# Reading a turned tile back from memory in quarters instead of halves

## The chip, the cores and the metric

The kernel runs on one core of a Trainium2 chip. The metric is the time of one execution in microseconds (us) on the device. The core has a matrix engine (PE, with weight loads shown as a row of their own, PEld), a vector engine (DVE), a scalar engine (ACT), a general engine (POOL), and a queue processor (SP) that issues DMA transfers and computes nothing. Transfers run on 16 DMA engines that all queues share.

## The reference, cut to what matters

```python
# attention: batch 8, heads 8, sequence 576, head size 64
scores = scale * q @ k.T
thresh = max(scores) - tau                      # along each row
scores = where(scores >= thresh, scores, -1e9)
attn   = softmax(scores)
x      = (attn @ v) as (4608, 512)              # tokens x (heads * 64)
# bilinear feed-forward: d_ff 1536
out    = ((x @ w_a) * (x @ w_b)) @ w_out
```

All of it is float32.

## The kernel before, in words

**Units and slots.** Two heads of one batch element form a pair; there are 32 pairs. A pair's 576 query rows are cut into four blocks of 128 rows (u = 0 to 3) and a rest of 64 rows; the rests of two neighbouring pairs are handled together as one block (u = 4, called NT). Each (pair, u) is a unit; there are 144 of them. The main loop runs over slots g = 0 to 146. In slot g the scores of unit g are made on PE (`scores`, line 404), reduced on DVE (line 411), exponentiated on ACT (432), masked and summed on DVE (435) and normalised on ACT (454).

**Turning the weights.** For attn @ v the weights must stand with the keys on the partitions. From slot 9 on this is done in two steps. DVE transposes within blocks of 32x32 (line 502). Then the blocks are exchanged through a buffer in device memory: in slot g `turn_blocks` posts four transfers of 144 KB that write unit g-1 to the buffer `swap` (shown as `swap<-tw`, one for each group of 32 partitions), and `turn_back` posts the transfers that read unit g-2 back into a tile `wT` (shown as `wT<-swap`). There are two `wT` tiles. Group y of the tile is read from block y of the buffer, which one of the four writes filled. Before it posts the reads, `turn_back` issues whatever is still waiting of that unit's writes (`flush`). The rests of units (NT) are read back by transfers of 144 KB of their own.

**Product.** `weighted` multiplies two units of a pair with v (`product`, line 546: 72 matmuls over two `wT` tiles, each of which reads from all four groups of one tile). It runs three slots after the second unit of the two. ACT and DVE copy the result out (553, 554), and the results of four pairs together are the input of the feed-forward, whose matmuls (lines 750, 854, 920) fill the slots between the attention parts. The order of PE's instructions is written out by the loop; `advance` hands out a number of columns of feed-forward work at fixed places of a slot.

**The queue of transfers.** Up to slot 36 `post` issues a transfer at once (line 144). From slot 37 on (`state["paced"]`) it appends it to a list, `bulk`, and transfers of the kinds "tw" and "wT" are put ahead of loads and stores that were posted in this slot or the one before. `passed` counts the columns that PE has been given, and takes the next entry from the list when the count has reached zero. An entry then costs 320 columns for each 36864 elements (144 KB) that it moves, rounded down, so that a load of k or q (under 144 KB) costs nothing. `pump` (line 157) issues the entry on SP, its first transfer behind the PE instruction last written, so that SP waits for that instruction's end. What is left in the list when a consumer is written is issued by `flush` without such a wait. SP executes strictly in order.

**Loads.** Four slots ahead of a pair's first unit its k is posted (four transfers of 72 KB), two slots ahead DVE transposes it (line 365); q follows in two parts, v in four transfers. They have the lower priority described above.

Of the kernel before, what the change touches and what calls it, by code (L numbers as in the profile page):

```python
# [54 lines left out]
def kernel(  # L55
# [57 lines left out]
    G = P // Q  # L113
# [25 lines left out]
    def post(key, *moves):  # L139

        if not state["paced"]:
            for move in moves:
                state["turn"] += state["over"]
                (nc.scalar if state["turn"] % 2 else nc.sync).dma_start(*move)  # L144
        else:
            at = len(bulk)
            if key[0] in ("tw", "wT"):
                while at and bulk[at - 1][0][0] not in ("tw", "wT") and bulk[at - 1][1] >= state["slot"] - 1:
                    at -= 1
            bulk.insert(at, (key, state["slot"], moves))  # L150
# [13 lines left out]
    def flush(*keys):  # L164

        while any(key in keys for key, _, _ in bulk):
            pump(1, False)
# [68 lines left out]
    for F in range(NF):  # L236
# [3 lines left out]
    state = {"loaded": 0, "added": 0, "converted": 0, "rows": 0, "sums": False, "through": 0, "over": False,  # L240
             "layer": False, "paced": False, "all": False, "turn": 0, "due": NPIECES, "wide": True, "slot": 0, "reading": False, "first": 0}
# [113 lines left out]
    prepared, scored, weights, turned, whole = {}, {}, {}, {}, {}  # L355
# [111 lines left out]
    def turned_tile(here=None):  # L467
        if here == (0, NT):
            return sums_sb[:, NSUM - TURNED:].rearrange("p (g s e) -> p g s e", g=G + 1, s=NSLOT)
        return work.tile([P, G + 1, NSLOT, Q], FP32, tag="wT", bufs=2, name="wT")  # L470
# [46 lines left out]
    def turn_back(i, u):  # L517

        key = "wT", i, min(u // 2, 1) if i >= HP else u // 2
        if u < NT or i < HP:  # L520
            flush(("tw", i, u))
            swap = swaps.pop((i, u)).rearrange("g p e -> p g e")
            turned[i, u] = turned_tile((i, u))
            for y in range(0, G, 2):
                post(key, (turned[i, u][:, y:y + 2].rearrange("p g s e -> p g (s e)"), swap[:, y:y + 2]))
        if i >= HP and u == (3 if i % 2 else NT):
            flush(("tw", i - i % 2, NT))
            swap = swaps[i - i % 2, NT].rearrange("g p e -> p g e")
            for y in range(2):
                post(key, (turned[i, 2 + y][:, G].rearrange("p s e -> p (s e)"), swap[:, i % 2 * 2 + y]))  # L530
            if i % 2:
                del swaps[i - 1, NT]
# [579 lines left out]
    n = 0  # L1112
# [4 lines left out]
    for g in range(len(units) + PV_LAG):  # L1117
# [9 lines left out]
        if BY_PE + 1 < g <= len(units) + 1:  # L1127
            n = g - PV_LAG
            back = (1 if BY_PE <= n and parts(*units[n]) else 0,)
            if not back[0] or units[g - 2] == (0, NT):  # L1130
                turn_back(*units[g - 2])
        if here:
            i, u = units[g]
# [38 lines left out]
        if g > BY_PE:  # L1172
            n = g - PV_LAG
            held = 0.0
            now = parts(*units[n]) if BY_PE <= n < len(units) else []
            if now:
                held = 384 - (PORTIONS[2] + PORTIONS[3]) * pace + NSLOT * sum(width(*x) for x in now) // 2
                held = min(max(held, 0.0), 384)
            advance(PORTIONS[1] * pace - held)
            for p in range(HP, NPR):  # L1180
                for name, d in (("k", 2),):
                    if g == (second if False else first)[p] - d:
                        prep(p, name)
            for p, h in now:
                if pairs[p][1] == 0:
                    make_x(2 if h == 1 and p >= HP and pairs[p][0] % GT == 0 else 1)
                make_room()
                weighted(p, h)
                passed(NSLOT * width(p, h) // 2)
                running["owed"] -= NSLOT * width(p, h) // 2  # L1190
            if back and back[0] > 0 and units[g - 2] != (0, NT):
                turn_back(*units[g - 2])
# [89 lines left out]
```

## Time and profile before

| | us |
|---|---|
| runs | 1406.40 (median), 1405.77, 1414.82 |
| profiled execution, whole | 1400.57 |
| its span, first to last instruction | 1398.8 |
| PE busy | 1361.5 |
| DVE busy | 1013.9 |
| ACT busy | 680.8 |

The profile is of one execution. "Busy" counts the time in which an engine has an instruction under way; PE's share says that it is nearly always occupied, not that it is at its peak. An entry of the waits names who waited, the line, who ended the wait, the total in us, how often, and the longest. SP computes nothing, so all of its rows are issues and waits, and its engine name carries a q (SPq). A row of an operation has the number of instructions and the shortest, median and longest duration in nanoseconds.

The transfers that the change touches run between 310 us (slot 37) and 1251 us. Of the reads into `wT` in that stretch, 194 move 288 KB and 50 move 144 KB (the rests).

### The profile page before, as it was taken

The numbers are of one execution on the slowest core, as the hardware profiler recorded it, in microseconds if no ns is written. First come the engines' busy times: TensorE is split into PE (matmuls) and PEld (weight loads), VectorE is DVE, ScalarE is ACT, GpSimd is POOL, SyncE is SP. The second block draws the span as 40 slices with busy tenths as digits, with TensorE's granted clock in tenths as the row PEclk, the third lists the DMA queues.
The fourth block names the chain that finished last, engine by engine and source line by source line (L and its number), as shares of the span: only waits on it lengthen the run. The fifth ranks groups of instructions, "written<-read, shape, count | busy, mean of one in ns | idle before, by whom it ended". The sixth has DMA issues, their size and how long they took to land.

```text
span 1398.8 us, 76307 instructions
## 1 busy us (share of the span) xinstructions
PE 1361.5 (97%) x33836; PEld 1258.5 (90%) x33836; DVE 1013.9 (72%) x2205; ACT 680.8 (49%) x1248; POOL 492.8 (35%) x675
## 2 busy tenths in 40 slices
PE   7889999999999999999999999999999999999998
PEld 5677588999998799999999999998899998799998
DVE  6999877787777768786767776778777776745425
ACT  6977555545554555544454545454545455431110
POOL 2764543424150607060515142332515060708100
PEclk9999999999999999999999999999999999999999
DMA  9977876667666775676556775566656775550000
GB/s 211 241 212 223 204 206 173 174 170 187 174 154 168 190 192 155 176 190 160 143 143 160 186 180 159 136 190 169 181 130 161 199 190 154 137 146 19 4 19 18
DMA packets 327449, 223.21 MB, mean 160 GB/s; under 512 B 171600, under 2 KB 311632, under 8 KB 327120
## 3 DMA queue, kind: packets, MB, share of 16 engines
q1 hardware_dynamic: 323936, 216.95, 60.1%
q8 instruction: 266, 4.36, 1.3%
q10 hardware_dynamic: 3184, 1.38, 0.4%
q14 instruction: 63, 0.52, 0.1%
HBM read 128.58 MB, written 89.65 MB: 156 GB/s over the span
## 4 chain that ended last, share of the span: by engine, by line
PE 88%; DMA 5%; DVE 4%; SPq 2%; issue 1%; ACT 1%; ACTq 0%; DVEq 0%
PE pab L750 29%; PE po L920 22%; PE pab L854 18%; PE sc L404 9%; PE pv L546 9%; SPq L144 1%; DMA vm<-in_v_dram 1%; DMA wT<-swap 1%; DVE tw L435 1%; DVE mx L411 1%; DMA more_u<-in_moe_w_a_dram 1%; DVE low L311 0%; DMA more_u<-in_moe_w_b_dram 0%; DVE tw L502 0%; DMA sums_u<-in_k_dram 0%
## 5 line engine op out<-in xcount | busy, mean ns | idle before, releaser
L454 ACT ACTIVATE tw<-tw,rcp 128x576 f32<-128x576 f32 x272 | 196.1, 768 | 201.3 <-DVE rcp L448 201.3
L411 DVE TENSOR_REDUCE mx<-sc 128x1 f32<-128x576 f32 x288 | 204.6, 752 | 121.2 <-PE sc L404 120.9
L432 ACT ACTIVATE tw<-sc,bias,scalars 128x576 f32<-128x576 f32 x288 | 239.6, 832 | 10.4 <-DMA qT<-in_q_dram 0.4
L712 POOL TENSOR_TENSOR h<-h,u 128x512 f32<-128x512 f32 x28 | 35.2, 1277 | 590.4 <-DVE h L824 414.1
L435 DVE SCALAR_TENSOR_TENSOR tw<-sc,thr,tw 128x576 f32<-128x576 f32 x288 | 220.9, 797 | 12.3 <-ACT tw L432 11.9
L920 PE MATMUL po<-wo_sb,h 64*64 64x256 f32 (+1 forms) x3408 | 210.5, 367 | 0.0
L502 DVE STREAM_TRANSPOSE tw<-tw 128x576 f32<-128x576 f32 x272 | 194.4, 752 | 0.8 <-ACT tw L454 0.8
L920 PEld LDWEIGHTS po<-wo_sb,h 64*64 64x64 f32 x3408 | 169.8, 133 | 14.9
L404 PE MATMUL sc<-kT,qT 64*64 64x288 f32 x2016 | 170.3, 404 | 1.8 <-issue 0.9
L546 PE MATMUL pv<-wT,vm 64*64 64x128 f32 (+2 forms) x4896 | 164.0, 275 | 3.7 <-DMA vm<-in_v_dram 1.4
L546 PEld LDWEIGHTS pv<-wT,vm 64*64 64x64 f32 x4896 | 153.2, 133 | 12.0 <-issue 4.0
L920 PE MATMUL po<-sums_u,h 64*64 64x256 f32 x2448 | 156.6, 376 | 0.0
L883 POOL TENSOR_TENSOR h<-h 128x256 f32<-128x256 f32 x168 | 117.2, 731 | 110.9 <-PE po L920 106.1
L750 PE MATMUL pab<-xU,wb_sb 64*64 64x128 f32 x4352 | 137.8, 269 | 0.0
L920 PEld LDWEIGHTS po<-sums_u,h 64*64 64x64 f32 x2448 | 126.1, 133 | 12.3 <-DVE h L862 0.5
L750 PEld LDWEIGHTS pab<-xU,wb_sb 64*64 64x64 f32 x4352 | 133.3, 133 | 1.8 <-ACT h L806 0.5
L404 PEld LDWEIGHTS sc<-kT,qT 64*64 64x64 f32 x2016 | 108.8, 133 | 17.3 <-issue 4.9
L431 ACT ACTIVATE bias<-mx,scalars 128x1 f32<-128x1 f32 x288 | 82.7, 287 | 66.1 <-DVE mx L411 65.6
L553 ACT COPY xT<-pv 128x128 f32<-128x128 f32 (+1 forms) x68 | 17.6, 259 | 193.5 <-PE pv L546 193.5
L750 PE MATMUL pab<-xS,wa_sb 64*64 64x128 f32 x2176 | 108.5, 269 | 0.8 <-issue 0.8
L554 DVE COPY xT<-pv 64x128 f32<-64x128 f32 (+1 forms) x136 | 38.1, 280 | 80.5 <-PE pv L546 79.0
L535 ACT COPY kept<-po 128x512 f32<-128x512 f32 x65 | 34.8, 535 | 120.3 <-PE po L920 106.4
(163 smaller groups left out, 2468.7 us busy)
## 6 DMA issues: line engine op xcount, KB each, us to landing
wT<-swap SPq DMA_DIRECT2D x242, 288.0 KB, 3.8
swap<-tw SPq DMA_DIRECT2D x480, 144.0 KB, 3.1
vm<-in_v_dram SPq DMA_DIRECT2D x128, 72.0 KB, 2.6
swap<-tw SPq DMA_DIRECT2D x128, 72.0 KB, 2.9
kT<-in_k_dram SPq DMA_DIRECT2D x112, 72.0 KB, 3.2
wT<-swap SPq DMA_DIRECT2D x56, 144.0 KB, 3.6
out_dram<-kept SPq DMA_DIRECT2D x27, 256.0 KB, 3.7
qT<-in_q_dram SPq DMA_DIRECT2D x112, 40.0 KB, 2.8
```

The lines of the kernel that those rows point to most:

```text
L404: nc.tensor.matmul(sc[m][o * D:o * D + wide, c], qT[r, q0:q0 + wide], kT[r, c * SH:(c + 1) * SH], start=True, stop=True)
L411: nc.vector.tensor_reduce(mx[:, c], sc[j], axis=AX.XY, op=ALU.max)
L431: nc.scalar.activation(bias[:, j:j + 1], mx[:, j:j + 1], AF.Copy, scale=e_nscale)
L432: nc.scalar.activation(wb[j], sb[j], AF.Exp, bias=bias[:, j:j + 1], scale=e_scale)
L435: nc.vector.scalar_tensor_tensor(out=wv, in0=sb[j], scalar=thr[:, j:j + 1], in1=wv, op0=ALU.is_ge, op1=ALU.mult, accum_out=sums[:, j:j + 1])
L454: nc.scalar.activation(w, w, AF.Copy, scale=rcp[:, j:j + 1])
L502: nc.vector.transpose(w, w)
L546: nc.tensor.matmul(pv[c * D:(c + 1) * D, y], vm[rows, s], wT[y](rows, s), start=(s == 0), stop=(s == NSLOT - 1))
L750: nc.tensor.matmul(out[c * D:(c + 1) * D, r, f * P:(f + 1) * P], w[g][k][rows, w0:w0 + D], moving[k][rows], start=(fresh and k == 0 and f ...
L854: nc.tensor.matmul(pab[c:c + columns(), r], w[rows, f // n, k, fs + c:fs + c + columns()], moving, start=(k == 0), stop=(k == H - 1))
L883: (nc.vector if state["over"] else nc.gpsimd).tensor_tensor(*a, **kw)
L920: nc.tensor.matmul(po[c * D:(c + 1) * D, r, y, cut], ht[rows, t0:t0 + D], other[rows, f, cut], start=(f == 0), stop=(f == NF // 2 - 1))
```

## The change

Inside `turn_back`, from slot 37 on, each of the four groups of a unit's tile is read back by a transfer of its own (144 KB) and posted as an entry of its own; up to slot 36 two groups go together as before (288 KB). The entries of the rests are as they were. Each entry costs 320 columns in place of 640, and each brings its own wait for a PE instruction.

```diff
             flush(("tw", i, u))
             swap = swaps.pop((i, u)).rearrange("g p e -> p g e")
             turned[i, u] = turned_tile((i, u))
-            for y in range(0, G, 2):
-                post(key, (turned[i, u][:, y:y + 2].rearrange("p g s e -> p g (s e)"), swap[:, y:y + 2]))
+            n = 1 if state["paced"] else 2
+            for y in range(0, G, n):
+                post(key, (turned[i, u][:, y:y + n].rearrange("p g s e -> p g (s e)"), swap[:, y:y + n]))
         if i >= HP and u == (3 if i % 2 else NT):
```

## The prediction

> **What bounds the kernel now.** I read the page first, then the stretch that the change touches (310 us, slot 37, to 1262 us, the last product) by windows, then the waits of PE and of SP in that stretch, then the rows of the tiles wT and kT and of line 546. The page's first part says which engine is full:
>
> ```profile
> PE 1361.5 (97%) x33836; PEld 1258.5 (90%) x33836; DVE 1013.9 (72%) x2205; ACT 680.8 (49%) x1248; POOL 492.8 (35%) x675
> ```
>
> That is a mean over stages. The windows give the stretch itself (length, then busy time of PE, PEld, DVE, ACT, POOL, the granted clock, the DMA engines' share, GB/s):
>
> ```profile
> 310.00:500.00 190.00, 188.93 (x4859) 171.08 (x4854) 146.89 (x327) 99.97 (x181) 70.94 (x109) 1.00 0.69 179
> 500.00:700.00 200.00, 199.57 (x5089) 193.20 (x5085) 148.25 (x327) 97.32 (x176) 68.50 (x104) 1.00 0.64 166
> 700.00:900.00 200.00, 199.32 (x5234) 195.49 (x5228) 143.22 (x315) 97.42 (x175) 58.58 (x86) 1.00 0.62 162
> 900.00:1100.00 200.00, 198.98 (x5129) 186.67 (x5125) 149.99 (x330) 101.56 (x184) 70.28 (x108) 1.00 0.65 168
> 1100.00:1262.00 162.00, 160.92 (x4183) 146.98 (x4178) 109.05 (x240) 72.79 (x133) 52.01 (x77) 1.00 0.59 159
> ```
>
> PE is busy for 188.93 + 199.57 + 199.32 + 198.98 + 160.92 = 947.7 of 952 us, at a granted clock of 1.00. Its idle time in the stretch is 4.3 us. The rest of PE's idle time (1398.8 - 1361.5 - 4.3 = 33 us) lies before 310 us or after 1262 us, where the change does nothing. The 4.3 us are the first bound on any gain. Busy is not the same as at its peak, but the long pieces of the chain that ended last run evenly (128 matmuls of line 920 in 6.91 us twice, 54.0 ns each), so little is hidden in them.
>
> SP is the queue that the change loads. Its waits in the same stretch:
>
> ```profile
> SPq L157 <- DVE tw L502: 112.0, 54, 6.5
> SPq L157 <- PE pab L750: 105.8, 162, 3.6
> SPq L157 <- PE po L920: 85.3, 144, 3.0
> SPq L157 <- PE pab L854: 54.0, 88, 3.8
> SPq L157 <- PE sc L404: 36.3, 54, 2.3
> SPq L157 <- DMA swap<-tw: 16.9, 32, 1.7
> ```
>
> These six rows are 410 us of 952 in which SP stood still because something was not ready yet: 43% of the stretch. Mostly it is ahead of the work, and held back on purpose by its PE markers.
>
> **The change part by part.**
>
> *More issues on SP.* 194 transfers of 288 KB become 388 of 144 KB: 194 issues more, two for each of 97 units. What one costs:
>
> ```profile
> L157 SPq DMA_DIRECT2D swap<-tw x480: 303/396/2307, 313.4 to 1242.1; - x160
> L157 SPq DMA_DIRECT2D wT<-swap x244: 326/382/1687, 310.4 to 1250.9; - x122
> ```
>
> The writes of 144 KB have a median of 396 ns, the reads (four in five of 288 KB) 382 ns: an issue costs the same whatever it moves. With the semaphore instruction and the gaps between, SP's timeline has four such writes in 1.78 us (834.12 us), 0.445 us each. So 194 x 0.445 = 86 us more, or 0.89 us for each unit of about 9.8 us (952 / 97). Against 410 us of waiting that fits, and 324 us would be left. Everything behind the reads in SP's order (the next unit's writes, k, q, v, the stores) can slip by up to 0.89 us in a unit, until SP comes to the next marker that it has to wait for. In the slot at 1116 us the four writes of 144 KB behind the reads take 3.32 us in place of 1.78, because one of them waits for PE's scores; such a wait swallows the 0.89 us whole, and k comes after it. Cost on the path: 0. If that cover were gone, see the first rival.
>
> *Later markers.* The first group goes at the same column as before, the second 320 columns later than it went, the third at the same column, the fourth 320 later. Columns pass at four matmuls per 128: line 750 runs 312 matmuls in 8.66 us (27.8 ns each), so 320 columns are 0.28 us. Where the count jumps by 576 columns behind the scores, or by 1152 behind a product, two or more entries go on one marker, so not every quarter has a marker to itself. The reader of the tile is the product. Against each product's start I set the landing, read issue by issue from the trace, of the last read that had landed: the smallest distances in the stretch are 1.1 us (1104.3) and 1.6 us (1088.5), the typical one 5 us. The last quarter is later by 0.28 us and 0.89 us of issuing at most, 1.2 us, and moves half the bytes. Only the tightest product can be touched at all. Cost: 0, with an upper end of about 0.1 us.
>
> *The transfers themselves.* Bytes, run lengths (1152 bytes) and the order of the bytes stay. The issues of the stretch show how little the size does to one transfer:
>
> ```profile
> wT<-swap SPq DMA_DIRECT2D x194, 288.0 KB, 3.7
> wT<-swap SPq DMA_DIRECT2D x50, 144.0 KB, 3.6
> ```
>
> 3.7 us to landing for 288 KB, 3.6 us for 144 KB: nearly all of it is a fixed delay or time in a queue. The Trainium skill ("DMA: Bandwidth & Descriptors", Anatomy of one DMA, and Rules for kernel authors) says the same more sharply, and against this change: each DMA pays about 2.0 us whatever it moves, and transfers are to be joined into larger ones. By its figure, if nothing overlapped, 194 more would be 388 us; this trace has several in flight at any time, so I do not add that.
>
> *A finer wait for the writes.* A half reads two blocks of the buffer and waits for both writes; a quarter waits for one. At 1113.7 us the first half went once the second write had landed, 1.3 us after the first one. So the first quarter can go earlier, and only the last waits for the last write. This is a gain where reads hang on writes; SP's waits for writes are 16.9 us in all, yet in PE's waits of the stretch no wT stands at all:
>
> ```profile
> PE pab L750 <- issue: 2.1, 5, 0.8
> PE pv L546 <- issue: 1.1, 2, 0.7
> PE sc L404 <- DVE xt L554: 0.5, 1, 0.5
> PE sc L404 <- DVE xT L554: 0.3, 1, 0.3
> ```
>
> So it ends at most 4.3 us, at least 0. I take 0.5 us gained, nearest to the two short waits that end with DVE.
>
> *More semaphores ahead of a product.* A product now depends on eight reads in place of four.
>
> ```profile
> L546 PEldq EVENT_SEMAPHORE  x131: 51/51/1900, 317.8 to 1257.4; - x131
> ```
>
> 131 such instructions stand before 49 products, 51 ns each at the median, two waits in an instruction at most in the trace. Four more waits are two more instructions: 98 x 51 ns = 5.0 us if all of it showed. The 131 that are there (6.7 us) show at most as the 2.6 us of "issue" before line 546's weight loads; matmuls queued ahead hide them. I take 0.
>
> *k comes later.* This is what is late next:
>
> ```profile
> DMA kT<-in_k_dram: 2.1, 4
> ```
>
> That is DVE's transpose of k (line 365), which waited four times in 22, the longest 0.80 us. By landings, 11 of the 22 have under 2 us to spare. If these all slipped by 0.89 us, what exceeds their spare time adds up to 4.4 us; by twice that, 11.7 us. Once such a wait reached PE: DVE waited 0.72 us at 1106.8, the copies of line 554 came late, and PE's scores lost 0.46 us at 1108.7. I take two more of that kind, 1 us; ends 0 and 12 us.
>
> **Sum.** 0 + 0 + 0 - 0.5 + 0 + 1 = +0.5 us on an execution of 1400.57 us (span 1398.8 and 1.8 around it). The runs' median is 1406.4, 5.8 us above that execution, so I forecast 1407 by the runs' scale.
>
> **The rivals.**
>
> *SP falls behind (slower).* In the slots crowded with k, q, v and stores, the two extra issues are not absorbed, and each slot's writes, and with them the next reads, start late. The place is SP's order between a unit's reads and the next marker; the price is 0.89 us for each slot in which SP does not stand still between; it decides once SP's waits in a slot are under 0.89 us. For it: the kT row above, and SP's timeline from 780 to 797 us, which has hardly a pause between groups of issues. Against it: 410 us of waits, 4.2 us per unit. If a quarter of the 97 units pay, 24 x 0.89 = 21 us: 1428. The rule of the Trainium skill named above ("DMA: Bandwidth & Descriptors") would come out on this side.
>
> *The finer wait pays (faster, but little).* All reads that hang on writes come early, kT with them, and PE's 4.3 us go: 1402. For it: the reads at 1113.7 us. Against it: PE waits for no wT.
>
> *The semaphores show (slower by little or more).* 5 us, and as much again if each also holds up the weight load behind it: 1411 to 1416.
>
> *It does nothing of the kind it says.* Markers coincide, quarters go in pairs as before, and only issues are added: 1406, inside the forecast.
>
> **How the numbers follow.** No change, with the last rival in it, has 0.59; the finer wait 0.14; SP behind 0.19; the semaphores 0.08. One per cent (14 us) is about what a measurement of this kernel can tell from no change, as its three runs span 9 us. Faster by over 1% would need three times PE's idle time: 0.03, taken from the finer wait. Slower by over 1% (above 1420.5): SP behind, and a small part of the semaphores, 0.21. Within: 0.76. The low end is the finer wait's 1402 less 3 us for a lucky set of runs, 1399; the high end takes in the semaphores, the 12 us of k and the lower part of SP behind: 1424.
>
> **What would show it.** Right: 388 reads of 144 KB beside the rests at about 0.38 us per issue; SP's waits of line 157 down by some 86 us; PE still busy for 947 us or so of the stretch; kT's waits a few us at most. Wrong: rows of PE waiting for wT, vm or DVE after kT; a stretch that is longer than 952 us by more than PE's busy time explains; or many more "issue" waits before line 546.

## The result and the profile after

The changed kernel takes 1420.31 us (median of 7 runs, 1415.89 to 1423.13); the kernel before takes 1406.40 us (7 runs, 1403.06 to 1414.82). The two medians are 13.9 us apart; the ratio on record, taken over the runs, is 1.0079, with a 95% interval of 1.0056 to 1.0103: about 11 us slower. A second comparison on another occasion gave 1.0088 (1.0058 to 1.0118). The change is slower by a little under 1%.

The profiled execution took 1416.46 us with a span of 1414.7 us, 15.9 us above the one of before (which, with 1400.57 us, lies below all seven runs above). To see where these are, I cut both spans at the same two matmuls, the first and the last of the stretch in which the change acts. The windows (length, busy time of PE, PEld, DVE, ACT, POOL, clock, DMA share, GB/s) of the kernel before and of the changed one:

```profile
306.20:1261.20 955.00, 950.73 (x24522) 896.54 (x24515) 699.84 (x1543) 471.23 (x850) 320.09 (x481) 1.00 0.64 167
```

```profile
306.80:1274.20 967.40, 956.29 (x24518) 905.24 (x24514) 700.57 (x1542) 470.47 (x850) 320.08 (x481) 1.00 0.64 165
```

The same work takes 967.4 in place of 955.0 us: 12.4 of the 15.9 us. Another 0.6 us lie ahead of the stretch and 2.9 us behind it, where the two programs are the same; those I put down to the two executions. The DMA engines' share and rate hardly moved. PE's idle time went from 4.3 to 11.1 us, and its busy time grew by 5.6 us although it does the same matmuls. So PE's idle time shows little more than half of the loss.

A part of the growth of busy time is the clock. The 1.00 of the windows is rounded; in the changed kernel's stretch there is one phase of 3.4 us at half clock, right behind an idle time of PE of 2.09 us:

```profile
817.80:821.20 3.40, 3.40 (x35) 2.35 (x34) 1.50 (x4) 1.44 (x2) 0.00 (x0) 0.50 0.80 200
```

The stretch of the kernel before has none. 3.4 us at half clock are 1.7 us lost, and the longest matmuls of line 404 (684 ns, 454 before) stand in this phase. The profiles of the experiments below with two markers, with the change and an early k, with k ahead of the second unit's reads without the change, and of the change once more have five more such phases in the stretch. All six begin 0.1 to 1.3 us after the end of an idle time of PE of 2.0 to 4.0 us. Four idle times of 2.2 to 2.6 us have none behind them, so not every one brings it. The other 3.9 us of the growth are not traced; matmuls that are counted as busy while they wait may be among them.

What ended the waits of PE in the stretch (engine, line, who ended the wait, us, times, longest; line numbers behind the change have moved by one):

```profile
PE sc L404 <- DVE xt L555: 2.8, 2, 2.6
PE sc L404 <- DVE xT L555: 2.2, 2, 2.1
PE sc L404 <- DVE h L816: 1.8, 1, 1.8
PE pv L547 <- issue: 1.5, 3, 0.7
```

PE waits for DVE, at the scores. And DVE, of all things that come from memory, waits for k:

```profile
DVE kT L365 <- DMA kT<-in_k_dram: 17.0, 8, 3.0
```

Before, this row was 2.1 us in four waits. One of the eight, from the chain of work that ended last (start, length, what):

```profile
807.03 5.16 DMA wT<-swap
812.19 0.02 issue
812.21 0.02 SPq L157
812.22 0.03 issue
812.25 3.71 DMA kT<-in_k_dram
...
816.08 0.78 DVE kT L365
...
817.62 2.10 PE sc L404 x13
```

SP's last issue of k came at 812.25 us, k landed 3.71 us later, DVE could transpose it at 816.08, the copies of the product behind the transpose came late, and PE's scores started at 817.62 after an idle time of 2.09 us.

Set unit by unit against the kernel before, by the end of each unit's scores, PE falls behind in four places: by 2.7 us up to 512 us of the changed kernel (two waits for k, at 475 and 491 us), by 3.9 us at 820 to 830 us (the wait above, with the 1.7 us of half clock), by 2.3 us at 963 us and by 2.1 us at 1124 us. Together these are 10.9 of the 12.4 us. The other three of the eight waits for k (626, 794 and 980 us) cost PE nothing that can be seen; the rest of the 12.4 us is steps of under 1 us in both directions.

SP itself waits less than before, but is far from full:

```profile
SPq L157 <- PE pab L751: 106.5, 188, 3.3
SPq L157 <- PE po L921: 76.3, 151, 2.9
SPq L157 <- DVE tw L502: 68.6, 26, 5.9
SPq L157 <- PE pab L855: 56.2, 89, 3.6
...
SPq L157 <- DMA swap<-tw: 0.4, 1, 0.4
```

All rows of line 157 together are 346 us, against 416 us before. Waits for landings of transfers fell too, from 18.1 us to 2.2 us, and a load of k takes 3.3 us from issue to landing in both kernels; so it is not that transfers land later after their issue. The loss is not an average one; it sits in a few crowded slots. The same slot in the timelines of SP, before and after (start, length from the first issue of a group to the end of its last, what):

```profile
794.37 2.01 SPq L157 DMA_DIRECT2D swap<-tw  x4
796.47 3.64 SPq L157 DMA_DIRECT2D wT<-swap  x4
800.21 2.01 SPq L157 DMA_DIRECT2D swap<-tw  x4
802.33 3.33 SPq L157 DMA_DIRECT2D kT<-in_k_dram  x4
```

```profile
799.62 2.66 SPq L157 DMA_DIRECT2D swap<-tw  x4
802.38 5.03 SPq L157 DMA_DIRECT2D wT<-swap  x8
807.51 1.88 SPq L157 DMA_DIRECT2D swap<-tw  x4
809.49 3.55 SPq L157 DMA_DIRECT2D kT<-in_k_dram  x4
```

The reads of two units stand one behind the other ahead of k, so k has four issues more in front of it, not two. From the first write to the first load of k it was 7.96 us, and now it is 9.87 us. Against the moment at which DVE was free for k (809.04 us before, 813.11 us after) the first write of the group is 1.2 us later as well, and so k's first issue is 3.1 us later. A comparison of the two programs shows that every load and every write hangs on the same PE instruction as before, so nothing but SP's time and the landings can have moved them.

The 22 loads of k in the stretch can be parted by how long SP waited, in the kernel before, between the first of the reads ahead of k and k's first issue (reads in the 14 us ahead of it, waits of over 0.2 us, read instruction by instruction from the trace). In 13 of them it was 2.1 us or more: there k's first issue comes 0.3 us later on average, against the moment at which DVE is free for k, and DVE waits once, 0.8 us. In the other nine it was under 2 us: there k comes 2.1 us later on average, and seven of DVE's eight waits, 16.3 of 17.0 us, belong to them.

### The profile page after: what moved, and what is told of

Same layout as the page of the kernel before. It is cut to its first block, busy times and chain, and to the rows that moved or that the text cites. A ratio compares the mean times of both kernels' runs of the same rounds, so it can differ in the third digit from the quotient of the medians.

```text
span 1414.7 us, 76741 instructions
## 1 busy us (share of the span) xinstructions
PE 1368.3 (97%) x33836; PEld 1263.8 (89%) x33836; DVE 1013.7 (72%) x2205; ACT 679.3 (48%) x1248; POOL 493.4 (35%) x675
## 4 chain that ended last, share of the span: by engine, by line
PE 89%; DMA 4%; DVE 4%; ACT 1%; issue 1%; SPq 1%; DVEq 0%; POOL 0%; ACTq 0%; POOLq 0%
PE pab L751 29%; PE po L921 21%; PE pab L855 18%; PE sc L404 10%; PE pv L547 9%; DMA kT<-in_k_dram 1%; DMA wT<-swap 1%; DMA vm<-in_v_dram 1%; PE tp L483 1%; SPq L144 1%; DVE mx L411 1%; DVE tw L435 0%; DVE low L311 0%; PE po L991 0%; PE tp L378 0%
## 5 line engine op out<-in xcount | busy, mean ns | idle before, releaser
L432 ACT ACTIVATE tw<-sc,bias,scalars 128x576 f32<-128x576 f32 x288 | 239.4, 831 | 10.9 <-DMA qT<-in_q_dram 0.6
L435 DVE SCALAR_TENSOR_TENSOR tw<-sc,thr,tw 128x576 f32<-128x576 f32 x288 | 220.9, 796 | 12.4 <-ACT tw L432 12.1
L921 PE MATMUL po<-wo_sb,h 64*64 64x256 f32 (+1 forms) x3408 | 214.1, 367 | 0.0
L404 PE MATMUL sc<-kT,qT 64*64 64x288 f32 x2016 | 177.9, 406 | 9.6 <-DVE xt L555 2.8
L921 PEld LDWEIGHTS po<-wo_sb,h 64*64 64x64 f32 x3408 | 175.2, 133 | 11.7 <-issue 0.5
L547 PE MATMUL pv<-wT,vm 64*64 64x128 f32 (+2 forms) x4896 | 168.6, 276 | 4.7 <-issue 1.7
L921 PEld LDWEIGHTS po<-sums_u,h 64*64 64x64 f32 x2448 | 129.6, 133 | 9.7 <-DVE h L863 0.5
L404 PEld LDWEIGHTS sc<-kT,qT 64*64 64x64 f32 x2016 | 111.8, 133 | 27.6 <-issue 10.3
L751 PE MATMUL pab<-xT,wa_sb 64*64 64x128 f32 x1856 | 93.1, 269 | 0.2 <-DVE kept L537 0.2
```

The source lines that it names most:

```text
L404: nc.tensor.matmul(sc[m][o * D:o * D + wide, c], qT[r, q0:q0 + wide], kT[r, c * SH:(c + 1) * SH], start=True, stop=True)
L432: nc.scalar.activation(wb[j], sb[j], AF.Exp, bias=bias[:, j:j + 1], scale=e_scale)
L435: nc.vector.scalar_tensor_tensor(out=wv, in0=sb[j], scalar=thr[:, j:j + 1], in1=wv, op0=ALU.is_ge, op1=ALU.mult, accum_out=sums[:, j:j + 1])
L547: nc.tensor.matmul(pv[c * D:(c + 1) * D, y], vm[rows, s], wT[y](rows, s), start=(s == 0), stop=(s == NSLOT - 1))
L751: nc.tensor.matmul(out[c * D:(c + 1) * D, r, f * P:(f + 1) * P], w[g][k][rows, w0:w0 + D], moving[k][rows], start=(fresh and k == 0 and f ...
L921: nc.tensor.matmul(po[c * D:(c + 1) * D, r, y, cut], ht[rows, t0:t0 + D], other[rows, f, cut], start=(f == 0), stop=(f == NF // 2 - 1))
```

## The experiments

Theory A: each added issue takes SP some 0.4 us; where reads of two units go ahead of k, k comes 1.7 us later, DVE waits for it, and PE for DVE. The rivals stand in the expectations.

**The same four transfers with two markers.** What the change adds, without the added waits for PE:

```diff
-            for y in range(0, G, n):
-                post(key, (turned[i, u][:, y:y + n].rearrange("p g s e -> p g (s e)"), swap[:, y:y + n]))
+            for y in range(0, G, 2):
+                post(key, *((turned[i, u][:, z:z + n].rearrange("p g s e -> p g (s e)"), swap[:, z:z + n])
+                            for z in range(y, y + 2, n)))
```

> The changed kernel, but the four reads of 144 KB of a unit are posted as two entries of two, so that there are two waits for PE as before and only the number and size of the transfers differ. Theory A (each added issue takes SP 0.43 us, so the loads of k behind the reads of two units go some 1.7 us later, DVE waits for k and PE for DVE): as slow as the change, 8 to 14 us above the kernel before, DVE waits for k of 12 to 20 us. Rival B (the two added waits for PE hold SP up): within 3 us of the kernel before, DVE waits for k of 2 to 5 us.

1415.49 us, ratio 1.0085 (1.0071 to 1.0100): as slow as the change. DVE's waits:

```profile
DVE kT L365 <- DMA kT<-in_k_dram: 15.5, 9, 4.5
```

Rival B falls: the added markers aren't needed for the loss.

**Issues without bytes.** The kernel before, with a transfer of 4 bytes behind each read:

```diff
             for y in range(0, G, 2):
-                post(key, (turned[i, u][:, y:y + 2].rearrange("p g s e -> p g (s e)"), swap[:, y:y + 2]))
+                tiny = [(scratch.tile([1, 1], FP32, tag="tiny", bufs=16, name="tiny"), tau)] if state["paced"] else []
+                post(key, (turned[i, u][:, y:y + 2].rearrange("p g s e -> p g (s e)"), swap[:, y:y + 2]), *tiny)
```

> The kernel before with its reads of 288 KB as they are, and behind each of them, on the same marker, a transfer of 4 bytes from one place in device memory to another that nobody reads: 194 issues more, as many as in the change, and hardly a byte. Theory A (SP's time for an issue): as slow as the change or a little less, 6 to 12 us above the kernel before, DVE waits for k of 8 to 17 us. Rival E (reads of 144 KB themselves move or land worse than those of 288 KB): within 3 us of the kernel before, DVE waits for k under 4 us.

1416.62 us, ratio 1.0070 (1.0045 to 1.0095); the runs scatter more than the others' (1403.63 to 1421.82 us). The row of the added transfers (x count: shortest, median, longest ns) and DVE's wait:

```profile
L157 SPq DMA_DIRECT2D tiny<-in_tau_dram x194: 558/572/767, 310.9 to 1259.5; - x194
```

```profile
DVE kT L365 <- DMA kT<-in_k_dram: 14.6, 7, 3.3
```

194 transfers that move nothing cost nearly what the change costs. Rival E falls: the reads may be as large as before, and k is late all the same. A product waits for four reads here as in the kernel before, so the added semaphores and later quarters (rival D below) aren't needed for the loss either. Each of these issues took SP longer (572 ns) than one of 144 KB (383 ns), so this is a somewhat larger dose per issue.

**One transfer for a unit.** `n = G if state["paced"] else 2`.

> From slot 37 on a unit is read back in one transfer of 576 KB: 97 issues fewer than before in place of 194 more. Theory A: SP is earlier by up to 0.43 us per unit, DVE waits for k fall below 2.1 us, and the time goes down by 0 to 3 us, since PE has 4.3 us of idle time in the stretch before. Rival C (the size of the transfers sets how soon tiles land, and large ones come late): PE waits for wT appear, and the time goes up by more than 5 us.

1407.21 us, ratio 1.0033 (1.0016 to 1.0050): 4 to 5 us slower, which neither side expected in this way. SP's waits of line 157 rose to 453 us, 37 more, so the issues were saved. The wait for k stayed at 2.1 us (two waits), and PE waits for no wT. What grew is this, in PE's waits:

```profile
PE pab L751 <- issue: 5.6, 8, 1.6
PE pv L547 <- issue: 2.5, 4, 0.8
PE sc L404 <- DVE xt L555: 1.6, 1, 1.6
```

"issue" had 2.1 and 1.1 us in these two rows before. It is a wait that the profile puts down to nobody. The five longest such stalls start 1.0 to 2.0 us behind the start of a packet of the queue that brings instructions (266 packets in an execution, one in 5 us), so it may be that PE's instructions come late when large transfers are under way. That is argued, not shown; the five longest of the kernel before lie much the same, 1.5 to 2.2 us behind such a packet. Theory A's gain from fewer issues did not come.

**k a slot earlier,** with the change and without it:

```diff
-            for name, d in (("q0", 3), ("k", 4), ("q1", 3)):
+            for name, d in (("q0", 3), ("k", 5), ("q1", 3)):
```

> The changed kernel with k posted five slots ahead of its pair in place of four. Theory A: DVE no longer waits for k (under 1 us), and the time is within 3 us of the kernel before. Rival D (the eight semaphores ahead of a product, or the later quarters, cost PE time of their own): it stays at least 5 us above the kernel before although DVE no longer waits for k.

> The kernel before with k posted five slots ahead in place of four. Theory A: the 2.1 us of waits for k go, the time falls by 0 to 2 us. It is the partner of the run before it: what that run has above this one is what the four reads cost apart from k. Theory A: under 3 us; rival D: over 5 us.

With the change 1411.10 us, ratio 1.0054 (1.0041 to 1.0068); without it 1409.59 us, ratio 1.0044 (1.0026 to 1.0061). No wait of DVE for k is left in either. The two ratios are 0.10% apart, 1.4 us, which by their intervals can be off by some 3 us: in this pair the four reads cost little, and the added semaphores ahead of a product are within that. But the early k itself costs 0.44%, where I had expected a gain. PE's waits with the change show what is late in its place:

```profile
PE pv L547 <- DMA swap<-tw: 2.1, 1, 2.1
PE pv L547 <- issue: 1.7, 3, 0.7
PE pv L547 <- DMA wT<-swap: 1.6, 1, 1.6
PE pv L547 <- DVE tw L435: 1.3, 1, 1.3
```

Now the products wait, since k goes ahead of reads that they need.

**k ahead of the second unit's reads only,** without the change and with it:

```diff
-                while at and bulk[at - 1][0][0] not in ("tw", "wT") and bulk[at - 1][1] >= state["slot"] - 1:
+                while at and bulk[at - 1][0][0] not in ("tw", "wT", "k") and bulk[at - 1][1] >= state["slot"] - 1:
```

> The kernel before, but reads and writes that are posted after a load of k are no longer put ahead of it, so k goes before the reads of the second of the two units in place of after them. Theory A: no wait for k (under 0.5 us); what comes late instead is the reads behind k: PE waits for wT of 1 to 5 us; the time within 5 us of the kernel before.

> The changed kernel with the same rule for k. Theory A (a crowded slot has no SP time left, so what goes earlier makes something else late): waits for k under 1 us, PE waits for wT of 3 to 8 us, the time 2 to 9 us above the kernel before and below the change. Rival G (k is the only load without spare time): the time within 2 us of the run before this one.

Without the change 1405.59 us, ratio 0.9999 (0.9983 to 1.0014); with it 1412.33 us, ratio 1.0056 (1.0037 to 1.0075). DVE waits for no k in either. PE waits for wT, without the change and with it:

```profile
PE pv L546 <- DMA wT<-swap: 2.4, 2, 2.0
```

```profile
PE pv L547 <- DMA wT<-swap: 3.9, 4, 1.7
```

The two are 0.57% apart, 8 us. Rival G falls: k is only the first that shows. When it is put ahead, reads come late: PE's waits for them are 1.5 us longer with the change. Where the rest of the 8 us went is not shown, and this pair doesn't exclude that a part is rival D's. The pair with k a slot early had only 1.4 us between its two kernels, so what the four reads cost seems to depend on what else has been given up: in that pair the products wait even without the change.

**Eight transfers for a unit.** Each group is read in two halves of 64 partitions:

```diff
-            for y in range(0, G, 2):
-                post(key, (turned[i, u][:, y:y + 2].rearrange("p g s e -> p g (s e)"), swap[:, y:y + 2]))
+            for y in range(0, G, 2 - state["paced"]):
...
+                for r in range(2):
+                    post(key, (turned[i, u][r * D:(r + 1) * D, y].rearrange("p s e -> p (s e)"), swap[r * D:(r + 1) * D, y]))
```

> From slot 37 on each unit is read back in eight transfers of 72 KB, each an entry of its own: 582 issues more than before, three times what the change adds, 2.6 us of SP per unit. Theory A: the delay grows faster than the number, since the spare time of k is used up: 30 to 80 us above the kernel before, waits for k and for wT on DVE and PE. Rival F (the cost is bounded, since SP has 410 us of waits in the stretch): under 20 us above.

1633.12 us, ratio 1.1623 (1.1601 to 1.1645), 228 us more and far over both expectations. Three things go beyond the dose. An entry of 72 KB costs no columns (the price is rounded down), so the eight go on one marker. And such an issue takes SP more time:

```profile
L157 SPq DMA_DIRECT2D wT<-swap x826: 369/547/1832, 312.4 to 1484.7; - x166
```

547 ns at the median, against 383 ns for a quarter over all 128 partitions. 582 issues more at 547 ns, and 194 at 164 ns more, are 350 us, nearly all of the 416 us that SP had to spare. And PE now often stands idle, and the granted clock in the stretch is 0.94 (1.00 before); 0.06 of its 1184 us are 71 us. Then everything waits:

```profile
DVE qT L365 <- DMA qT<-in_q_dram: 75.3, 11, 9.9
DVE kT L365 <- DMA kT<-in_k_dram: 72.7, 10, 9.9
...
PE pv L550 <- DMA wT<-swap: 54.1, 30, 4.7
```

It shows the direction, and that the cost grows steeply once SP's spare time is nearly used up; as a measure of the number alone it is not clean.

**k from ACT's queue,** without the change and with it, and k and v without it:

```diff
-        if not state["paced"]:
+        if state["paced"] and key[0] in BY_ACT:      # ("k",), or ("k", "v")
+            for move in moves:
+                nc.scalar.dma_start(*move)
+        elif not state["paced"]:
```

> The kernel before, but from slot 37 on k is issued by ACT's queue when it is posted, with no marker; four issues per pair less on SP and k out of SP's order. Theory A (SP's order is what makes k late, and SP's time in the crowded slots is what is short): waits for k gone, no new PE waits for wT, time 0 to 4 us below the kernel before. Rival H (issuing costs ACT as much as it saves SP): ACT's exponentials come late, DVE and PE with them, 3 us or more above.

> The changed kernel with k issued by ACT in the same way. Theory A: within 4 us of the run before it, DVE waits for k under 2 us, so most of the change's 11 us goes. Rival D (the four reads cost in another place): still 6 us or more above the run before it.

> The kernel before with k and v issued by ACT: eight issues per pair less on SP. Theory A: as the run with k alone or up to 2 us faster. Rival H: 4 us or more above the kernel before.

1421.84 us (1.0131, 1.0108 to 1.0154), 1439.69 us (1.0259, 1.0235 to 1.0283) and 1425.03 us (1.0155, 1.0133 to 1.0176). Rival H holds: DVE no longer waits for k, but ACT stands still while it issues, behind landings of earlier transfers. An issue waits until the last transfer that used its completion semaphore has landed (there are eight, used in turn), and ACT does nothing else meanwhile. In the longest wait without the change the four issues of k start at 803.08, 805.95, 806.96 and 808.68 us, behind the landing of a load of v, a store and two writes to the buffer; each issue also takes ACT 0.64 us (median of 84). ACT's waits without the change and with it (the profile books them under k):

```profile
ACT bias L435 <- DMA kT<-in_k_dram: 9.1, 2, 4.8
ACT kept L539 <- DMA kT<-in_k_dram: 2.6, 1, 2.6
```

```profile
ACT bias L435 <- DMA kT<-in_k_dram: 19.1, 4, 7.3
ACT h L865 <- DMA kT<-in_k_dram: 5.8, 2, 3.3
```

The pair doesn't separate theory A from rival D as it was meant to. The kernels are 18 us apart, as D would have it, but ACT's own waits doubled between them (11.7 to 24.9 us), so the four reads cost there too, by way of ACT.

**The change once more.**

> The changed kernel once more, beside the others on their chip: 8 to 14 us above the kernel before, DVE waits for k of 12 to 20 us in a second profile.

1415.98 us, ratio 1.0088 (1.0058 to 1.0118); DVE waits 13.3 us for k in eight waits. In sum, 194 more issues on SP are enough for the loss: with two markers in place of four, and with hardly a byte and no added semaphore, k is late and the time as long. No version tried beats the kernel before; putting k ahead of the second unit's reads equals it.

## Why the prediction was right and where it was not

*The outcome.* The ratio lies within the 1% that I gave the greatest chance, and the time lies within the range, at its upper part. That is luck in part: the median of 1420.31 us is 0.2 us under the 1420.5 above which I had counted it as over 1%. The sum said +0.5 us, and about 11 us were measured, with an interval that excludes no change. What happened is the mechanism of the first rival, at half its price (21 us), with k as what comes late.

*What bounds the kernel* was right: PE does, and the change can only cost by making it wait.

*More issues on SP* had nearly the right price (a median of 383 ns measured, 0.38 us forecast; SP's waits fell by 70 us in a stretch that is 12.4 us longer, so SP's own time grew by about 82 us, 86 forecast), and the wrong conclusion, "cost on the path: 0". The median leaves out that one issue in ten takes over 1 us: the mean of the reads is 484 ns. I spread 0.89 us over every unit and showed one slot, at 1116 us, in which a wait for PE swallows it. That slot is the kindest of the 22: k comes 1.5 us earlier there than before, against DVE. In the slots in which SP hardly waits between the reads and k, nothing swallows the added time. The average of 410 us said nothing on those. That an issue costs the same whatever it moves held for 288 and 144 KB only: in the same trace a load of k (72 KB) has a median of 582 ns.

*k comes later* is the term that was mis-sized. It named the row, the place and the path, down to the copies of line 554 and the scores, and took 1 us of an interval from 0 to 12. DVE's waits rose from 2.1 to 17.0 us and the stretch grew by 12.4 us. Two things were wrong in it. The reads of two units go ahead of k, so the shift is four issues; on the 11 loads that had under 2 us to spare, k landed 1.8 us later on average against the time at which DVE was ready, where the "twice that" of the working was 1.78 us and gave 11.7 us. One by one they differ widely, from 0.8 us earlier to 3.7 us later, so the agreement is partly chance. And I let two waits more reach PE, with 1 us; five of the eight did (13.0 us of DVE's waiting), and PE lost 10.9 us there, 1.7 us of them by the halved clock, which the prediction had not counted.

*Later markers* cost nothing that the runs show, as forecast: PE waits for no wT in the changed kernel, and the run with two markers is as slow.

*The transfers themselves* were right in not counting: landing went from 3.7 us for 288 KB to 3.1 us at the median of all reads of the stretch. The Trainium skill ("DMA: Bandwidth & Descriptors", Rules for kernel authors) advises to join transfers. The trace agrees that more transfers cost; here it was SP's 0.4 us each, in order. The 2 us that the prediction quoted are no measure of it: the section Anatomy of one DMA gives them for transfers issued by the general engine, and these are issued by SP. Joining further, to 576 KB, did not pay (1.0033).

*A finer wait for the writes* did what was said on SP, whose waits for writes fell from 16.9 to 0.4 us, and brought PE nothing, as PE never waited for wT in the stretch before. The 0.5 us credited were wrong.

*More semaphores ahead of a product:* there are 199 in place of 131, fewer than the 229 worked out.

```profile
L547 PEldq EVENT_SEMAPHORE  x199: 51/51/1906, 318.3 to 1270.7; - x199
```

The 1.4 us between the two kernels with k a slot early, with some 3 us either way, are what the runs say of their cost. The rival of 1411 to 1416 us came nearer to the measured time than the forecast, but for another reason.

*That the change does nothing of the kind it says* falls with its time: the markers are indeed without effect, but issues alone cost 10 us (the run with 4 bytes).

## What to carry to other kernels

As far as this case goes, a queue that executes in order is not judged by its average idle time, but by the slots in which it doesn't stand still between the added instruction and the next load that has little to spare. Before splitting a transfer, list what is queued behind it, count the issues of all entries that go together there, and compare with the spare time of that load; if it is used up, most of the added delay can reach the bounding engine (10.9 of 13.0 us in the five waits that did). Moving the load ahead did not pay where the slot itself was full: what it passed became late.

## What the runs showed that I had not expected

The time SP needs for an issue goes neither by bytes nor simply by pieces: 383 ns for 144 KB over 128 partitions, 382 ns at the median when most reads were of 288 KB, 547 ns for 72 KB over 64 partitions, 572 ns for 4 bytes from device memory to device memory. A load issued by ACT stops ACT until earlier transfers have landed, 9.1 us in two waits; that cost more than SP's lateness. An idle time of PE of some 2 us can cost more than itself: six times a phase of 3.4 us at half clock, 1.7 us of work, came with it. And fewer, larger transfers cost 4 to 5 us, with longer "issue" waits of PE whose cause stays open.
